# Experts' first layer with one 512-column product for the high and low parts of the tokens

## The chip, the cores and the metric

The kernel runs on one core of one Trainium2 chip. The metric is device time in microseconds (us) for one execution, as the median of several runs.

## What is computed

A recurrence over 768 steps (4 batches, 8 heads of 48) gives 3072 rows of 384 numbers, and a mixture of experts with one expert per token is applied to them:

```python
for t in range(S):
    y[:, :, t] = einsum('bhd,bhde->bhe', r_t, state + (u * k_t) v_t^T)
    state = w_t[..., None] * state + k_t v_t^T
x = y.transpose(0, 2, 1, 3).reshape(3072, 384)
do_compute = x @ w_skip > 0              # the other rows pass through
e_idx = argmax(x @ w_gate)               # 8 experts
h = maximum(x[mask] @ w1[e], 0.0)        # 384 -> 1024
y[mask] = gate_w * (h @ w2[e])           # 1024 -> 384
out[do_compute] = x + y
```

## The kernel before

The first half (to about 132 us) is the recurrence in 24 chunks of 128 steps, with the router beside it. Each chunk's rows are stored to `out`; the router then gives each expert a table of up to 256 rows, in two halves of 128. The second half, `expert(e)` for e = 0 to 7 (L808 to L882), works through the experts one after another. Expert 0's first half of rows is done early, so expert 0 here has only its second half. The order on TensorE, ScalarE, VectorE and GpSimd is the order in which the program issues the work (`manual_schedule`); SP issues its transfers in program order too.

All products of an expert are made in three parts for precision: a number is split into a high part (a rounded copy, type fp32r) and a low part (what is left), and high x high, high x low and low x high are summed in PSUM.

**First layer** (experts 1 to 7, L821 to L851). The 1024 hidden units are done in eight blocks of 128, q = 0 to 7. A block is nine products of 256 columns (the 256 tokens): for each of the three pieces kc of the 384 inputs, w1h with xTh (L837), w1h with xTl (L838), w1l with xTh (L839). They are summed in a PSUM tile psH. The psH tiles go round four banks (tags psA0, psA1, psY, psB), so block q uses the bank of block q-4. Then ScalarE makes the high part of the hidden units, hh (L844, with the relu), and VectorE the low part, hl (L849), which is the last to read the bank.

**Weights of the next expert.** SP loads raw weights in pieces of 512 KB (`load_weights`, L84): three for the first layer into a buffer r0, three for the second into r1. They are cut into twelve slices of 128x512; `split_slice` (L92) makes the high part of one on ScalarE (L89, a cast) and the low part on VectorE (L90). Slices 0 to 5 are the first layer's (slice 2 kc + 0 or 1 holds the lower or upper half of the blocks for piece kc), 6 to 11 the second layer's. `more(k)` does k slices: one after each block, two after each half of the second layer. There is one r0 and one r1, so the load for expert e+2 waits until the slices of expert e+1 have been read out of the buffer.

**Tokens.** `tokens(e+1)` (L764) stands between the layers: six transposes on TensorE (L770) and the split of the next expert's tokens into xTh (ScalarE) and xTl (VectorE).

**Second layer** (L857 to L875). For each half j of the tokens, 24 products of 384 columns (L861 to L863); then VectorE computes fin (L870) from psO, the gate and the gathered rows xg, and GpSimd scatters fin to `out` (L775).

**GpSimd's queue.** Rows xg are gathered by GpSimd (L713), a pair of gathers per expert (`pair`). From expert 3 on a pair is paced: it waits for an hh of expert 0 or 1. The pairs of experts 6 and 7 wait for hh 0 and hh 1 of expert 1. Scatters are held back in `first` until all gathers are issued, and the first one waits until they have landed, since both touch `out`.

Of the kernel before, what the change touches and what calls it, by code (L numbers as in the profile page):

```python
# [8 lines left out]
F32 = mybir.dt.float32  # L9
BF16 = mybir.dt.bfloat16  # L10
F32R = mybir.dt.float32r
# [3 lines left out]
AF = mybir.ActivationFunctionType  # L15
ALU = mybir.AluOpType
# [5 lines left out]
P = 128  # L22
# [6 lines left out]
KC = DM // P  # L29
FC = DF // P  # L30
CAP = 256
# [25 lines left out]
def rwkv_moe_kernel(ctx, tc, wrk, wrk0, vN, uP, wgs, wgp, w12, cst, out):  # L57
    nc = tc.nc
# [13 lines left out]
    def wtile(e, k):  # L72
        nm = f"{WN[k]}{e % 2}"
        pool = wset0 if nm in ("w1h1", "w1l1", "w2h0", "w2l0") else wset1[0]
        t = wsp[e, k] = pool.tile([P, KC * DF], F32R, tag=nm, name=f"{nm}_{e}")
        return t
# [11 lines left out]
    def split(dst_h, dst_l, src, eng=None):  # L88
        nc.scalar.copy(dst_h, src)  # L89
        (eng or nc.vector).tensor_tensor(dst_l, src, dst_h.bitcast(F32), op=ALU.subtract)  # L90

    def split_slice(e, i, eng=None):  # L92
        q, cs = i // 6, slice((i % 6) * 512, (i % 6 + 1) * 512)
        for k in (2 * q, 2 * q + 1):
            if (e, k) not in wsp:
                wtile(e, k)
        split(wsp[e, 2 * q][:, cs], wsp[e, 2 * q + 1][:, cs], raws[e, q][:, cs], eng)
# [13 lines left out]
    def drain(g):  # L111
        for _ in g:
            pass
# [11 lines left out]
    def hidden(ps, xT, fc, kc):  # L125
        o = kc * DF + fc * P
        return nc.tensor.matmul(ps, raws[0, 0][:, o:o + P], xT[:, kc], start=(kc == 0),  # L127
                                stop=(kc == KC - 1))

    banks = ExitStack()  # L130
    ps1 = banks.enter_context(tc.tile_pool(name="ps1", bufs=1, space=PSUM))


    with tc.tile_pool(name="att", bufs=2) as att, \
# [477 lines left out]
        with tc.manual_schedule():  # L612
# [3 lines left out]
            for s in range(-2, n + 1):  # L616
# [73 lines left out]
                k = s + 1 - W_AT  # L690
# [19 lines left out]
        def gather(s, pool):  # L710
            if pool:
                xg[s] = pool.tile([P, DM], F32, tag=f"xg{s}", name=f"xg{s}", bufs=1)
            return nc.gpsimd.indirect_dma_start(  # L713
                out=xg[s], out_offset=None, in_=out,
                in_offset=bass.IndirectOffsetOnAxis(ap=idr[:, s % 2, s // 2:s // 2 + 1], axis=0),
                bounds_check=NT - 1, oob_is_err=False)
# [4 lines left out]
        with tc.manual_schedule(engines={nc.tensor.engine, nc.scalar.engine, nc.vector.engine}):  # L721
            todo, due, done = early_expert(), HEAD * STEP, [0]
# [21 lines left out]
    with tc.tile_pool(name="wset1", bufs=1) as ws1, tc.tile_pool(name="moe", bufs=2) as moe, \  # L744
            tc.tile_pool(name="ps2", bufs=1, space=PSUM) as ps2:
        wset1[0] = ws1
        def pair(e, instr=None):
            for s in (2 * e, 2 * e + 1):
                ga = gather(s, moe)
                if instr is not None:  # L750
                    tc.add_manual_dep(ga.ins, instr.ins.name,
                                      mybir.DependencyInfo(mybir.DependencyClass.Sync,
                                                           mybir.DependencyReason.DATA),
                                      reason="pace")
# [3 lines left out]
        later_pairs = list(range(3, E))  # L758
        verdicts = []
        first = []  # L760

        xTs = {}

        def tokens(e):  # L764
            xTh = moe.tile([P, KC, CAP], F32R, tag="xTh", name=f"xTh{e}")
            xTl = moe.tile([P, KC, CAP], F32R, tag="xTl", name=f"xTl{e}")
            for j in range(2):
                ps = ps1.tile([P, KC, P], F32, tag="psT", name=f"psX2{e}_{j}", bufs=2)
                for kc in range(KC):
                    nc.tensor.transpose(ps[:, kc], xg[2 * e + j][:, kc * P:(kc + 1) * P], ident)  # L770
                split(xTh[:, :, j * P:(j + 1) * P], xTl[:, :, j * P:(j + 1) * P], ps)
            xTs[e] = xTh, xTl

        def scatter(s, o):
            sc = nc.gpsimd.indirect_dma_start(  # L775
                out=out, out_offset=bass.IndirectOffsetOnAxis(ap=ids[:, s % 2, s // 2:s // 2 + 1],
                                                               axis=0),
                in_=o, in_offset=None, bounds_check=NT - 1, oob_is_err=False)
            tc.declare_no_dep(sc.ins, group="rows", reason="tokens are scattered to rows of their own")
            tc.add_to_no_dep_group("rows", sc.ins)  # L780
# [27 lines left out]
        def expert(e):  # L808
            todo = []
            if e + 1 < E:  # L810
                todo = list(range(0 if e > 0 else 6, 12))

            def more(k):
                for _ in range(k):
                    if todo:
                        split_slice(e + 1, todo.pop(0))


            h = {}
            nh = FC if e > 0 else FC // 2  # L820
            for q in range(nh):  # L821
                ps = (ps1 if q % 4 < 2 else ps2).tile(
                    [P, CAP], F32, tag=("psA0", "psA1", "psY", "psB")[q % 4], name=f"psH{e}_{q}")
                hh = moe.tile([P, CAP], F32R, tag="hh", name=f"hh{e}_{q}", bufs=NHB)
                hl = moe.tile([P, CAP], F32R, tag="hl", name=f"hl{e}_{q}", bufs=NHB)
                if e == 0:
                    for i in range(2):
                        ts = slice(i * P, (i + 1) * P)
                        for kc in range(KC):
                            hidden(ps[:, ts], xT0[1], 2 * q + i, kc)  # L830
                        h[1, 2 * q + i] = hh[:, ts], hl[:, ts]
                else:
                    w1h, w1l = wsp[e, 0], wsp[e, 1]
                    xTh, xTl = xTs[e]
                    for kc in range(KC):
                        o = kc * DF + q * P
                        nc.tensor.matmul(ps, w1h[:, o:o + P], xTh[:, kc], start=(kc == 0), stop=False)  # L837
                        nc.tensor.matmul(ps, w1h[:, o:o + P], xTl[:, kc], start=False, stop=False)  # L838
                        nc.tensor.matmul(ps, w1l[:, o:o + P], xTh[:, kc], start=False,  # L839
                                         stop=(kc == KC - 1))  # L840
                    for j in range(2):
                        ts = slice(j * P, (j + 1) * P)
                        h[j, q] = hh[:, ts], hl[:, ts]
                act = nc.scalar.activation(hh, ps, AF.Relu)  # L844
                if later_pairs and (e, q) != (0, 0):
                    pair(later_pairs.pop(0), act)
                    while first and not later_pairs:
                        scatter(*first.pop(0))
                nc.vector.scalar_tensor_tensor(hl, ps, 0.0, hh.bitcast(F32),  # L849
                                               op0=ALU.max, op1=ALU.subtract)  # L850
                more(1)  # L851
            if e + 1 < E:
                tokens(e + 1)
            if e == 0:
                first.append((0, fin0))
            w2h, w2l = wsp[e, 2], wsp[e, 3]
            for j in range(1 if e == 0 else 0, 2):  # L857
                pso = ps1.tile([P, DM], F32, tag=("psu", "pss")[j], name=f"psO{e}_{j}")
                for fc in range(FC):
                    o = slice(fc * DM, (fc + 1) * DM)  # L860
                    nc.tensor.matmul(pso, h[j, fc][0], w2h[:, o], start=(fc == 0), stop=False)  # L861
                    nc.tensor.matmul(pso, h[j, fc][0], w2l[:, o], start=False, stop=False)  # L862
                    nc.tensor.matmul(pso, h[j, fc][1], w2h[:, o], start=False,  # L863
                                     stop=(fc == FC - 1))
                more(2)
                if j == 0 and e in (1, 2):
                    (row_tests, verdict)[e - 1]()
                s = 2 * e + j
                o = moe.tile([P, DM], F32, tag="fin", name=f"fin{e}_{j}", bufs=3)
                nc.vector.scalar_tensor_tensor(o, pso, gates[:, j, e:e + 1], xg[s],  # L870
                                               op0=ALU.mult, op1=ALU.add)
                if later_pairs:
                    first.append((s, o))
                else:
                    scatter(s, o)  # L875
                if s == 2 * E - 3:
                    nc.gpsimd.drain()
                    verdicts.append(nc.values_load(flag_i[0:1, 0:1], min_val=0, max_val=2))
            more(12)
            if e + 2 < E:  # L880
                drain(load_weights(e + 2, 0))
                drain(load_weights(e + 2, 1))  # L882
# [170 lines left out]
```

## Time and profile before

| | |
|---|---|
| median of 3 runs | 289.99 us (289.51 to 290.56) |
| the profiled execution's own time | 289.28 us |
| its span, first to last instruction | 287.5 us |
| mean granted TensorE clock | 0.996 |
| TensorE busy | 269.7 us, 94% of the span |
| VectorE busy | 215.6 us, 75% |
| ScalarE busy | 160.7 us, 56% |
| GpSimd busy | 145.6 us, 51% |

The page calls TensorE's matmuls PE and its weight loads PEld, VectorE DVE, ScalarE ACT, GpSimd POOL and SyncE SP. A matmul's duration in a row is longer than its pitch, since matmuls are pipelined: what one costs in a row of them is the distance from its start to the next one's start. "L837" is line 837 of the kernel before. In a row `psH<-xTh,w1h` the tile before the arrow is written and those behind it are read. An entry in brackets at a row's end is the time that the engine sat idle before it, and what ended it.

### The profile page before, as it was taken

How to read it: one execution, taken by the hardware profiler on the slowest of the kernel's cores; microseconds unless marked ns; L12 is line 12 of the kernel's file. 1: busy time of each engine (PE TensorE's matmuls, PEld its weight loads, DVE VectorE, ACT ScalarE, POOL GpSimd, SP SyncE). 2: the span in 40 equal slices, each digit the busy share in tenths (PEclk: the TensorE clock that was granted, in tenths of full speed). 3: DMA queues.
4: the chain of work that ended last, by engine and by line, in shares of the span. 5: the costliest groups of instructions: out<-in, count | busy, mean ns of one | idle time of the engine just before them, and what ended most of it. 6: DMA issues, size and time to landing. Idle time of an engine off the chain costs nothing.

```text
span 287.5 us, 8933 instructions
## 1 busy us (share of the span) xinstructions
PE 269.7 (94%) x3587; PEld 247.9 (86%) x3588; DVE 215.6 (75%) x412; ACT 160.7 (56%) x466; POOL 145.6 (51%) x140
## 2 busy tenths in 40 slices
PE   6899999999999998989889999999999999999993
PEld 2688888878887887877889999999999999999992
DVE  7998899999999999852638596966859578595420
ACT  5266656786767855967327481835728367282310
POOL 4987775699979996983566635011020110301111
PEclk9999999999999999999999999999999999999998
DMA  7999999987998779962365997566562656600001
GB/s 221 225 319 354 332 324 378 357 255 245 280 330 263 240 239 377 275 219 84 126 214 167 359 342 240 199 227 235 198 231 78 235 225 217 247 25 27 8 3 43
DMA packets 26131, 64.41 MB, mean 224 GB/s; under 512 B 4342, under 2 KB 15386, under 8 KB 26080
## 3 DMA queue, kind: packets, MB, share of 16 engines
q1 hardware_dynamic: 23712, 58.14, 60.9%
q0 software_dynamic: 2048, 5.48, 5.8%
q8 instruction: 30, 0.49, 0.7%
q10 hardware_dynamic: 320, 0.13, 0.2%
q14 instruction: 21, 0.17, 0.2%
HBM read 56.69 MB, written 7.86 MB: 225 GB/s over the span
## 4 chain that ended last, share of the span: by engine, by line
issue 33%; PE 11%; POOL 6%; DVE 4%; ACT 2%; DMA 1%; POOLq 1%; DVEq 0%
POOL out L775 5%; PE psH L127 2%; DMA xg<-out,idr 1%; PE psH L839 1%; PE psH L838 1%; PE psH L837 1%; DVE w2l L90 1%; PE psY L395 1%; PE psA L344 1%; PE psY L363 1%; ACT w1h L107 1%; PE psO L862 0%; PE psO L861 0%; PE psO L863 0%; DVE hot L488 0%
## 5 line engine op out<-in xcount | busy, mean ns | idle before, releaser
L775 POOL DMA_INDIRECT out<-fin,ids x16 | 16.8, 1048 | 99.8 <-DVE fin L870 94.0
L844 ACT ACTIVATE hh<-psH 128x256 fp32r<-128x256 f32 x60 | 23.0, 384 | 57.6 <-PE psH L839 54.3
L839 PE MATMUL psH<-xTh,w1l 128*128 128x256 f32 x168 | 47.5, 283 | 0.0
L838 PE MATMUL psH<-xTl,w1h 128*128 128x256 f32 x168 | 47.5, 283 | 0.0
L837 PE MATMUL psH<-xTh,w1h 128*128 128x256 f32 x168 | 47.5, 283 | 0.0
L861 PE MATMUL psO<-w2h,hh 128*128 128x384 f32 x120 | 40.9, 341 | 0.0
L863 PE MATMUL psO<-w2h,hl 128*128 128x384 f32 x120 | 40.2, 335 | 0.0
L862 PE MATMUL psO<-w2l,hh 128*128 128x384 f32 x120 | 40.1, 334 | 0.0
L312 POOL TENSOR_TENSOR kq<-wrk,q 128x512 f32<-128x512 f32 x24 | 28.4, 1184 | 13.9 <-DVE q L295 5.2
L350 DVE TENSOR_TENSOR asb<-psA,c_sb 128x512 f32<-128x512 f32 x48 | 30.5, 677 | 4.7 <-PE psA L344 4.6
L849 DVE SCALAR_TENSOR_TENSOR hl<-psH,hh 128x256 fp32r<-128x256 f32 x60 | 25.2, 420 | 11.5 <-ACT hh L844 10.0
L317 DVE TENSOR_TENSOR_SCAN rh<-wrk,rowsk,pss 128x520 f32<-128x520 f32 x24 | 31.1, 1296 | 3.2 <-PE pss L537 1.0
L295 DVE TENSOR_TENSOR_SCAN q<-wrk,pss 128x520 f32<-128x520 f32 x24 | 29.6, 1232 | 3.6 <-DMA wrk<-wrk 1.1
L839 PEld LDWEIGHTS psH<-xTh,w1l 128*128 128x128 f32 x168 | 32.2, 192 | 0.0
L838 PEld LDWEIGHTS psH<-xTl,w1h 128*128 128x128 f32 x168 | 32.2, 192 | 0.0
L837 PEld LDWEIGHTS psH<-xTh,w1h 128*128 128x128 f32 x168 | 32.2, 191 | 0.0
L304 POOL TENSOR_TENSOR rk<-wrk 128x512 f32<-128x512 f32 x24 | 31.2, 1298 | 0.8 <-DMA wrk<-wrk 0.8
L322 POOL TENSOR_TENSOR rp<-wrk,rh 128x512 f32<-128x512 f32 x23 | 27.3, 1187 | 6.0 <-DVE rh L317 5.5
L395 PE MATMUL psY<-asb,v 128*48 128x128 f32 x384 | 26.5, 276 | 3.8 <-DVE psY L367 3.8
L870 DVE SCALAR_TENSOR_TENSOR fin<-psO,gates,xg 128x384 f32<-128x384 f32 x15 | 9.3, 618 | 27.4 <-PE psO L863 23.1
L90 DVE TENSOR_TENSOR w2l<-r,w2h 128x512 fp32r<-128x512 f32 x42 | 27.8, 687 | 0.9
L344 PE MATMUL psA<-rp,kq 64*64 64x64 f32 (+1 forms) x768 | 25.8, 251 | 2.2 <-DVE rp L322 1.4
(151 smaller groups left out, 603.7 us busy)
## 6 DMA issues: line engine op xcount, KB each, us to landing
r<-w SPq DMA_DIRECT2D x48, 512.0 KB
wrk<-wrk SPq DMA_DIRECT2D x21, 772.5 KB
v<-vN SPq DMA_DIRECT2D x24, 192.0 KB
vt<-wrk SPq DMA_DIRECT2D x48, 96.0 KB
out<-x SPq DMA_DIRECT2D x24, 192.0 KB
wrk<-wrk SPq DMA_DIRECT2D x1, 579.4 KB
wrk<-wrk SPq DMA_DIRECT2D x1, 512.0 KB
wrk<-wrk SPq DMA_DIRECT2D x1, 384.0 KB
```

The costliest lines, as they stand in the source:

```text
L90: (eng or nc.vector).tensor_tensor(dst_l, src, dst_h.bitcast(F32), op=ALU.subtract)
L295: nc.vector.tensor_tensor_scan(q.rearrange("p a j -> p (a j)")[:, ::-1], t[:, 1:1 + n_][:, ::-1], ones_at[:, 1:1 + n_][:, ::-1], 0.0, op0= ...
L304: nc.gpsimd.tensor_tensor(work[i]["rk"].rearrange("p a j -> p (a j)"), t[:, R_OFF:K_OFF], t[:, K_OFF:V_OFF], op=ALU.mult)
L317: nc.vector.tensor_tensor_scan(rh.rearrange("p a j -> p (a j)"), wk["w"][:, 0:NP * CW], reads_at[:, :NP * CW], rowsk, op0=ALU.mult, op1=AL ...
L350: nc.vector.tensor_tensor(s, psa[g], tri.rearrange("p (o j) -> p o j", o=1).to_broadcast([P, NP, P]), op=ALU.mult)
L775: sc = nc.gpsimd.indirect_dma_start(out=out, out_offset=bass.IndirectOffsetOnAxis(ap=ids[:, s % 2, s // 2:s // 2 + 1], axis=0), in_=o, in_ ...
L837: nc.tensor.matmul(ps, w1h[:, o:o + P], xTh[:, kc], start=(kc == 0), stop=False)
L838: nc.tensor.matmul(ps, w1h[:, o:o + P], xTl[:, kc], start=False, stop=False)
L839: nc.tensor.matmul(ps, w1l[:, o:o + P], xTh[:, kc], start=False, stop=(kc == KC - 1))
L861: nc.tensor.matmul(pso, h[j, fc][0], w2h[:, o], start=(fc == 0), stop=False)
L862: nc.tensor.matmul(pso, h[j, fc][0], w2l[:, o], start=False, stop=False)
L863: nc.tensor.matmul(pso, h[j, fc][1], w2h[:, o], start=False, stop=(fc == FC - 1))
```

## The change

In the first layer the tokens' high and low parts lie side by side in one tile xT. One product of w1h with both, 512 columns wide, takes the place of L837 and L838 and fills a whole bank: its left half collects high x high, its right half high x low. The product of w1l with the high part is added into the left half. ScalarE copies the right half to SBUF (`side`), and VectorE adds it to the left half in PSUM; then hh and hl follow as before, out of a function `finish`, which is called one block later. The splitting of the next expert's weights moves: in the first layer of experts 1 to 6 one slice after every second block (0, 2, 4, 6), the first of them on VectorE and the low parts of the other three on GpSimd, and four instead of two after each half of the second layer.

```diff
         def tokens(e):
-            xTh = moe.tile([P, KC, CAP], F32R, tag="xTh", name=f"xTh{e}")
-            xTl = moe.tile([P, KC, CAP], F32R, tag="xTl", name=f"xTl{e}")
+            xT = moe.tile([P, KC, 2, CAP], F32R, tag="xT", name=f"xT{e}")
+            xTh, xTl = xT[:, :, 0], xT[:, :, 1]
...
-            def more(k):
+            def more(k, eng=None):
                 for _ in range(k):
                     if todo:
-                        split_slice(e + 1, todo.pop(0))
+                        split_slice(e + 1, todo.pop(0), eng)
+
+            def finish(q, ps, hh, hl):
+                act = nc.scalar.activation(hh, ps, AF.Relu)
+                if later_pairs and (e, q) != (0, 0):
+                    pair(later_pairs.pop(0), act)
+                    while first and not later_pairs:
+                        scatter(*first.pop(0))
+                nc.vector.scalar_tensor_tensor(hl, ps, 0.0, hh.bitcast(F32),
+                                               op0=ALU.max, op1=ALU.subtract)
+                if e == 0 or q % 2 == 0:
+                    more(1, nc.gpsimd if e > 0 and q > 0 else None)
 
-            h = {}
+            h, due = {}, []
             nh = FC if e > 0 else FC // 2
             for q in range(nh):
-                ps = (ps1 if q % 4 < 2 else ps2).tile(
-                    [P, CAP], F32, tag=("psA0", "psA1", "psY", "psB")[q % 4], name=f"psH{e}_{q}")
+                both = (ps1 if q % 4 < 2 else ps2).tile(
+                    [P, 2, CAP], F32, tag=("psA0", "psA1", "psY", "psB")[q % 4], name=f"psH{e}_{q}")
+                ps = both[:, 0]
...
                     for kc in range(KC):
                         o = kc * DF + q * P
-                        nc.tensor.matmul(ps, w1h[:, o:o + P], xTh[:, kc], start=(kc == 0), stop=False)
-                        nc.tensor.matmul(ps, w1h[:, o:o + P], xTl[:, kc], start=False, stop=False)
-                        nc.tensor.matmul(ps, w1l[:, o:o + P], xTh[:, kc], start=False,
-                                         stop=(kc == KC - 1))
+                        nc.tensor.matmul(both, w1h[:, o:o + P], xT[:, kc], start=(kc == 0),
+                                         stop=(kc == KC - 1), skip_group_check=True)
+                        nc.tensor.matmul(ps, w1l[:, o:o + P], xT[:, kc, 0], start=False,
+                                         stop=(kc == KC - 1), skip_group_check=True)
+                    side = moe.tile([P, CAP], F32, tag="side", name=f"side{e}_{q}")
+                    nc.scalar.copy(side, both[:, 1])
+                    nc.vector.tensor_tensor(ps, ps, side, op=ALU.add)
...
-                act = nc.scalar.activation(hh, ps, AF.Relu)
-                if later_pairs and (e, q) != (0, 0):
-                    pair(later_pairs.pop(0), act)
-                    while first and not later_pairs:
-                        scatter(*first.pop(0))
-                nc.vector.scalar_tensor_tensor(hl, ps, 0.0, hh.bitcast(F32),
-                                               op0=ALU.max, op1=ALU.subtract)
-                more(1)
+                due.append((q, ps, hh, hl))
+                if e == 0 or q > 0:
+                    finish(*due.pop(0))
+            while due:
+                finish(*due.pop(0))
...
-                more(2)
+                more(4)
```

On ScalarE, at the beginning of expert 2's first layer, the order before was (hh is the high part of the hidden units, w1h_3 the high part of expert 3's first-layer weights, r_30 the raw ones):

```order
L844 ACTIVATE hh_0_3163<-psH_0_3162 128x256
L89 CAST w1h_3_3176<-r_30_3154 128x512
L844 ACTIVATE hh_1_3181<-psH_1_3180 128x256
L89 CAST w1h_3_3176<-r_30_3154 128x512
L844 ACTIVATE hh_2_3197<-psH_2_3196 128x256
```

and now it is:

```order
L854 COPY side_0_3169<-psH_0_3160 128x256
L854 COPY side_1_3181<-psH_1_3172 128x256
L820 ACTIVATE hh_0_3161<-psH_0_3160 128x256
L89 CAST w1h_3_3186<-r_30_3152 128x512
L854 COPY side_2_3199<-psH_2_3190 128x256
L820 ACTIVATE hh_1_3173<-psH_1_3172 128x256
```

The cast of slice 0 now stands ahead of the copy of block 2 and of hh 1.

On GpSimd, from expert 1 on, the order before was scatters alone (fin_73 and fin_1_2898 are expert 0's two halves):

```order
L775 DMA out<-fin_73,ids 3072x384
L775 DMA out<-fin_1_2898,ids 3072x384
L775 DMA out<-fin_0_3115,ids 3072x384
L775 DMA out<-fin_1_3149,ids 3072x384
L775 DMA out<-fin_0_3341,ids 3072x384
```

and now it is (w1l_2 is the low part of expert 2's first-layer weights, r_20 the raw ones):

```order
L775 DMA out<-fin_73,ids 3072x384
L775 DMA out<-fin_1_2897,ids 3072x384
L90 TENSOR_TENSOR w1l_2_2942<-r_20_2899,w1h_2_2941 128x512 x3
L775 DMA out<-fin_0_3109,ids 3072x384
L775 DMA out<-fin_1_3147,ids 3072x384
L90 TENSOR_TENSOR w1l_3_3187<-r_30_3152,w1h_3_3186 128x512 x3
```

Three low parts per expert stand between the scatters of the expert before and its own. On SP, the load of expert 3's raw first-layer weights had these waits before:

```order
L84 DMA r_30_3154<-w 128x1024 [waits DMAHW1_49,DMAHW2_49,DMAHW0_49,DVE_49]
L84 DMA r_30_3154<-w 128x1024 x2
```

and has these now:

```order
L84 DMA r_30_3152<-w 128x1024 [waits DMAHW1_49,DMAHW0_49,DMAHW2_49,DVE_49,Pool_49]
L84 DMA r_30_3152<-w 128x1024 x2
```

GpSimd (Pool) has come in beside VectorE among those that the load waits for.

## Rows read from the trace of the kernel before

**Rows 1.** Busy time by stretch, PE to POOL; then granted clock, DMA share, GB/s

```profile
149.00:282.30 133.30, 133.30 (x959) 132.95 (x958) 90.28 (x178) 67.96 (x152) 28.72 (x27) 1.00 0.51 180
212.60:221.20 8.60, 8.60 (x73) 8.60 (x73) 7.17 (x14) 6.30 (x14) 0.98 (x1) 1.00 0.48 181
```

**Rows 2.** Timeline of PE: expert 0's second layer, experts 1 and 4 (start, us, engine, line)

```profile
155.33 0.34 PE L862 MATMUL psO<-w2l,hh 128*128 128x384 f32 x1
...
159.15 0.33 PE L863 MATMUL psO<-w2h,hl 128*128 128x384 f32 x1
159.32 0.28 PE L837 MATMUL psH<-xTh,w1h 128*128 128x256 f32 x1
...
212.59 0.28 PE L837 MATMUL psH<-xTh,w1h 128*128 128x256 f32 x1
...
221.21 0.82 PE L770 MATMUL psX<-c_sb,xg 128*128 128x128 f32 x6
...
230.21 0.28 PE L837 MATMUL psH<-xTh,w1h 128*128 128x256 f32 x1
```

**Rows 3.** Timeline of PE, warm-up products (the second is the third after the first)

```profile
5.28 0.59 PE L610 MATMUL psw<-warm 128*128 128x512 bf16 x2
...
5.92 0.59 PE L610 MATMUL psw<-warm 128*128 128x512 bf16 x2
```

**Rows 4.** Timeline of ACT, first activation of expert 4

```profile
213.85 0.38 ACT L844 ACTIVATE hh<-psH 128x256 fp32r<-128x256 f32 x1 [6.34 <-PE psH L839]
```

**Rows 5.** Groups by line: VectorE's product in PSUM, of the recurrence

```profile
L367 DVE TENSOR_TENSOR psY<-psY,vt 128x512 f32<-128x512 f32 x24 | 16.6, 690 | 0.0
```

**Rows 6.** Timeline of ACT, then of DVE, expert 1

```profile
161.70 0.39 ACT L844 ACTIVATE hh<-psH 128x256 fp32r<-128x256 f32 x1 [4.31 <-PE psH L839]
161.98 0.61 ACT L89 CAST w1h<-r 128x512 fp32r<-128x512 f32 x1
162.49 0.39 ACT L844 ACTIVATE hh<-psH 128x256 fp32r<-128x256 f32 x1
...
161.57 0.62 DVE L870 SCALAR_TENSOR_TENSOR fin<-psO,gates,xg 128x384 f32<-128x384 f32 x1 [3.13 <-PE psH L839]
162.12 0.43 DVE L849 SCALAR_TENSOR_TENSOR hl<-psH,hh 128x256 fp32r<-128x256 f32 x1
162.62 0.69 DVE L90 TENSOR_TENSOR w1l<-r,w1h 128x512 fp32r<-128x512 f32 x1
163.23 0.42 DVE L849 SCALAR_TENSOR_TENSOR hl<-psH,hh 128x256 fp32r<-128x256 f32 x1
163.57 0.68 DVE L90 TENSOR_TENSOR w1l<-r,w1h 128x512 fp32r<-128x512 f32 x1
```

**Rows 7.** Timeline of POOL (low parts, gathers, scatters) and the PE row that waited

```profile
136.51 3.71 POOL L108 TENSOR_TENSOR w1l<-r,w1h 128x512 fp32r<-128x512 f32 x3 [0.97 <-ACT w1h L107]
143.80 1.21 POOL L713 DMA_INDIRECT xg<-out,idr  x1 [3.58 <-DMA r<-w]
...
147.95 0.52 PE L572 MATMUL psX<-c_sb,xg 128*128 128x128 f32 x3 [0.86 <-DMA xg<-out,idr]
...
166.73 1.23 POOL L713 DMA_INDIRECT xg<-out,idr  x1 [0.30 <-issue]
173.15 1.02 POOL L775 DMA_INDIRECT out<-fin,ids  x1 [5.19 <-DVE good L790]
174.47 1.00 POOL L775 DMA_INDIRECT out<-fin,ids  x1 [0.30 <-DVE vt L799]
```

**Rows 8.** Timeline of SP: issues of raw weights

```profile
140.25 0.34 SPq L84 DMA_DIRECT2D r<-w  x1
...
168.05 1.46 SPq L84 DMA_DIRECT2D r<-w  x2
...
220.90 0.33 SPq L84 DMA_DIRECT2D r<-w  x1
```

**Rows 9.** DMA queues from 168 to 172 us: packets, MB, share of 16 engines

```profile
q1 hardware_dynamic: 194, 0.71, 49.7%
q0 software_dynamic: 176, 0.51, 40.6%
```

More of the change, by code (lines that the diff above doesn't have):

```diff
@@ L771, in tokens @@
                 split(xTh[:, :, j * P:(j + 1) * P], xTl[:, :, j * P:(j + 1) * P], ps)
-            xTs[e] = xTh, xTl
+            xTs[e] = xT
         def scatter(s, o):
@@ L833, in expert @@
                     w1h, w1l = wsp[e, 0], wsp[e, 1]
-                    xTh, xTl = xTs[e]
+                    xT = xTs[e]
                     for kc in range(KC):
                         o = kc * DF + q * P
-                        nc.tensor.matmul(ps, w1h[:, o:o + P], xTh[:, kc], start=(kc == 0), stop=False)
-                        nc.tensor.matmul(ps, w1h[:, o:o + P], xTl[:, kc], start=False, stop=False)
-                        nc.tensor.matmul(ps, w1l[:, o:o + P], xTh[:, kc], start=False,
-                                         stop=(kc == KC - 1))
+                        nc.tensor.matmul(both, w1h[:, o:o + P], xT[:, kc], start=(kc == 0),
[5 more added lines that the diff above has]
+                    nc.vector.tensor_tensor(ps, ps, side, op=ALU.add)
                     for j in range(2):
```

## The prediction

> **What bounds the kernel now.** I read the busy times by stretch first. From 149.0 to 282.3 us TensorE is busy all the time, at a granted clock of 1.00 (the full 2.4 GHz), while VectorE is busy 68% and ScalarE 51% of it [rows 1]; in an expert's first layer VectorE has 7.17 of 8.60 us. Next the timeline of TensorE. Expert 4 begins at 212.59, ends its first layer at 221.21 and hands over to expert 5 at 230.21 [rows 2]: 8.62 us for 72 products of 256 columns, one per 119.7 ns, with no gap. So here the end of the kernel is a sum of product pitches, and whatever shortens a pitch shortens the kernel, as long as nobody makes TensorE wait. The start and the recurrent part are the same in both orders and drop out.
>
> **The products.** What has to be known is the pitch of a 512-column product of this type; the trace has none. It has 256 columns at 119.7 ns and 384 columns at (159.15 - 155.33)/22 = 173.6 ns [rows 2], so 128 columns more cost 53.9 ns, and 512 columns come to 173.6 + 53.9 = 227.5 ns. Two bounds: twice the short one, 239.4 ns (nothing saved), and the bf16 512-column warm-up products, (5.92 - 5.28)/3 = 213 ns [rows 3]. I take 227.5, because the 384-column row is of the same type with a weight load each and is the nearest. One merge saves 239.4 - 227.5 = 11.9 ns; 24 per expert and seven experts make 168: **-2.0 us** (0 to -4.4 by the bounds). The 168 weight loads that go are overlapped by products and gain nothing of their own.
>
> What does a fixed cost per product look like elsewhere? The Trainium skill ("TensorE: Matmul & The Clock Gate", section "Back-to-back issue gap") gives a gap of N / 2.4 + 2.5 ns; 256 columns would take 109.2 ns, against 119.7 in the trace. By that page a merge would save 2.5 ns and all of them an estimated 0.42 us. The sum here does not use it.
>
> **The added work and the ring of four banks.** Per block of 128 hidden units there is one more copy on ScalarE (the side, PSUM to SBUF, 128x256: like the 0.38 us activation of that size [rows 4]) and one more add on VectorE in PSUM. A 128x512 VectorE product in PSUM takes 690 ns [rows 5]; at half the columns I take 0.43, close to the 0.42 of the hl row [rows 6], with 0.38 and 0.69 as ends. Three of the four low parts that the first layer still splits go to GpSimd at 1.26 us each. By load this fits: on one engine the next instruction starts 0.28 us after an activation and 0.51 after a cast, 0.34 after hl and 0.61 after a low part [rows 6]; ScalarE has 16 x 0.28 + 4 x 0.51 = 6.5 us and VectorE 16 x 0.35 + 0.61 = 6.2 us in a layer of 8 x 1.04 = 8.34 us.
>
> The latency is tighter. A bank is written by TensorE, read by side, rewritten by the add, read by hh and hl, and TensorE wants it back four blocks later. Before, hh starts 1.26 us after the layer's start [rows 4], 0.18 after the next block begins; a hop from ScalarE to VectorE costs 0.03 [rows 6]. In the new order, from the layer's start: side 1 at 2 x 1.04 + 0.18 = 2.26, hh 0 at 2.54, the cast of slice 0 at 2.82, its low part on VectorE 3.48; side 2 at 3.34; add 2 behind the low part at 4.09; hl 1 at 4.44, over at 4.86. TensorE asks for bank 1 at 5.21: a margin of 0.3 us. The later blocks come out at 0.6. No wait in an ordinary expert.
>
> Expert 1 is not ordinary. Its first activation starts at 161.70 and fin at 161.57, 1.1 us later than 159.32 + 1.26 [rows 2, 6]; the old order, with one step fewer in the ring, absorbed it. In the new one: side 0 at 2.38, add 0 2.80, hh 0 3.27, cast 3.55, low part 4.21, add 2 4.82, hl 1 from 5.17 to 5.59, bank back at 5.64 against 5.21: **+0.4 us** (0 if the late start does not recur).
>
> **What is moved past a queue.** This is the step I weigh most. In expert 1 GpSimd's queue holds four gathers, which wait for hh 0 and hh 1, then two scatters, which wait until the gathers have landed. The three low parts of expert 2 now stand behind those scatters; they were on VectorE. Before, the last gather was started at 166.73 and took 1.23 us, and the first scatter started at 173.15 [rows 7]. Two things hang on the three low parts. TensorE needs slice 2 at the second low product of expert 2. And SP's load of expert 3's raw first-layer weights goes into the buffer they read, so it waits for the third; before, it was issued at 168.05 [rows 8], right behind the sixth low part on VectorE.
>
> In the new order hh 0 of expert 1 ends at 159.32 + 3.65 = 162.97; the gathers follow at 1.3 us and the last is over at 168.1 to 168.8. When does it land? The fastest seen is 2.9 us (end of the 143.80 gather to the product that waited for it at 147.95), the slowest the 5.2 to the scatter at 173.15 [rows 7]. So the first scatter starts between 171.3 and 174.0. I take 172.0, nearer the early end: from 168 to 172 the weight load took 49.7% of the DMA engines beside the gathers' 40.6% [rows 9], and in the new order that load is not there yet. Two scatters at 1.3 and three low parts, the row of three taking 3.71 us [rows 7], end at 172.0 + 2.6 + 3.7 = 178.3 (177.6 to 180.3). A raw piece is ready 3.2 us after its issue (issue at 140.25 [rows 8]; the gather at 143.80 that waited for it, less 0.3): 181.5.
>
> Expert 2 starts at 159.32 + 17.62 - 0.29 + 0.43 = 177.1 and wants to cast slice 0 at 177.1 + 2.82 = 179.9. ScalarE takes its work in order, so side 2 stands behind that cast, add 2 and hl 1 behind side 2; bank 1 is free 2.1 us after the piece: 183.6, and TensorE wants it at 177.1 + 5.21 = 182.3: **+1.3 us** (0.6 to 3.3). Slice 2's low part, at 177.1, is in time for 177.7, barely.
>
> From expert 2 on the scatters come later than the low parts, so GpSimd is free. The raw load of an expert's successor is issued when slices 4 and 5 are split, behind the tokens, some 12.6 us into the expert (before: 8.3, at 220.90 [rows 8]), and is wanted 20.2 us in: with 3.2 us to land that costs nothing; without those 4 us of cover each expert would stall as expert 2 does. The second raw half is issued behind fin as before and wanted 3 us later than before: nothing.
>
> **Sum.** -2.0 + 0.4 + 1.3 = -0.3 us, on the profiled execution's 289.28 us 289.0; the median of the runs is 289.99, 0.7 above it, so I predict 289.7 us. **No change that can be measured**: 0.3% of the time, 0.87 us, is what a measurement here can tell from none.
>
> **Rivals.**
> - **The late load does not show (faster).** If gathers land fast, or GpSimd's third low part is over by 177.0, only expert 1's wait is left: -1.6 us, 288.4; without that wait too, 288.0. For it: the DMA engines are emptier then. Against it: even 2.9 us of landing leaves 0.6 us of wait. Chance 0.32, with the partial forms of it that still gain over 0.87.
> - **The late load shows fully (slower).** Gathers land as late as before: low parts over at 180.3, expert 2 waits 3.3 us, sum +1.7, 291.7. It decides from 179.5 on for the third low part. For it: the gathers start 0.9 us later than before and their own backlog is the same. Chance 0.18.
> - **The pitch goes by columns, nothing is fixed (slower).** 512 columns take 239 ns; then only the waits are left: +1.7, 291.7. The 384-column row speaks against it (it would be 179.6, and is 173.6). A page's 2.5 ns, above, would make 291.3 of it. Chance 0.08.
> - The forecast, within 0.87 us of before: 0.42.
>
> A fourth, inside the slower ones: the in-place add costs its 512-wide 0.69 us. Then the 0.3 us margin of every expert goes too.
>
> **Numbers.** Faster 0.32, same 0.42, slower 0.18 + 0.08 = 0.26. The range runs from the two clean forms (288.0) to just under the two slow ones (291.6), with the tails of each, at most 0.2, left outside.
>
> **What would show it.** The 512-column product starts 227 ns before its follower; the first layers of experts 3 to 7 take 8.34 us without a gap. TensorE has one gap of some 0.4 us at block 5 of expert 1 and one of 1.3 us at block 5 of expert 2. GpSimd's three low parts of expert 2 start behind two scatters at about 174.6, and SP issues the following raw load at 178.3. Wrong I would be if that load is issued before 177 or its cast does not hold ScalarE, if the gaps recur in each expert, or if the 512-column pitch is 213 or 239.

## The result and the profile after

The changed kernel takes **292.81 us** (median of 6 runs, 292.42 to 293.32) against 290.27 for the kernel before (6 runs): a ratio of 1.0088, 95% interval 1.0067 to 1.0109. It is slower by 2.5 us, above the forecast of 289.7 and outside the range of 288.0 to 291.6. The profiled execution took 292.42 us with a span of 290.6 and a mean granted clock of 0.989 (before: 289.28, 287.5, 0.996).

First the groups by line of the changed kernel (line, engine, operation, count | busy us, mean ns of one | idle time ahead and its releaser). They answer to [rows 4, 5]:

```profile
L849 PE MATMUL psH<-xT,w1h 128*128 128x512 f32 x168 | 60.7, 402 | 3.0 <-DVE hl L825 2.7
L855 DVE TENSOR_TENSOR psH<-psH,side 128x256 f32<-128x256 f32 x56 | 23.9, 431 | 17.3 <-ACT side L854 16.6 <-issue 0.5 <-ACT w1h L89 0.2
L854 ACT COPY side<-psH 128x256 f32<-128x256 f32 x56 | 21.0, 376 | 40.5 <-PE psH L851 37.1 <-ACT side L854 2.7 <-issue 0.4
L795 DVE TENSOR_SCALAR good<-gall 128x24 f32<-128x24 f32 x1 | 4.1, 4149 | 0.0
```

All 168 merged products are there, and the added copy (376 ns) and add (431 ns) cost what was put in the sum. The odd row is the last: a VectorE instruction on 128x24 numbers that took 4149 ns.

The timeline of PE, which answers to [rows 2] (start, us, engine, line; idle time and releaser in brackets), in experts 2 and 3:

```profile
176.56 0.39 PE L849 MATMUL psH<-xT,w1h 128*128 128x512 f32 x1
176.79 0.28 PE L851 MATMUL psH<-xT,w1l 128*128 128x256 f32 x1
176.91 0.39 PE L849 MATMUL psH<-xT,w1h 128*128 128x512 f32 x1
177.38 0.39 PE L851 MATMUL psH<-xT,w1l 128*128 128x256 f32 x1
...
181.02 0.28 PE L851 MATMUL psH<-xT,w1l 128*128 128x256 f32 x1
184.04 0.50 PE L849 MATMUL psH<-xT,w1h 128*128 128x512 f32 x1 [2.74 <-DVE hl L825]
...
185.08 0.28 PE L851 MATMUL psH<-xT,w1l 128*128 128x256 f32 x1
185.48 0.80 PE L849 MATMUL psH<-xT,w1h 128*128 128x512 f32 x1
...
186.28 0.63 PE L849 MATMUL psH<-xT,w1h 128*128 128x512 f32 x1
186.71 0.41 PE L851 MATMUL psH<-xT,w1l 128*128 128x256 f32 x1
...
188.84 0.39 PE L849 MATMUL psH<-xT,w1h 128*128 128x512 f32 x1
...
190.25 0.49 PE L770 MATMUL psX<-c_sb,xg 128*128 128x128 f32 x3
...
199.65 0.39 PE L849 MATMUL psH<-xT,w1h 128*128 128x512 f32 x1
...
207.97 0.82 PE L770 MATMUL psX<-c_sb,xg 128*128 128x128 f32 x6
```

Expert 3's first layer takes 207.97 - 199.65 = 8.32 us, as do those of experts 4 to 7. Expert 2's takes 190.25 - 176.56 = 13.69. Of the excess of 5.37, 0.24 lie where the second low product came 0.47 instead of 0.23 us behind its neighbour, **2.90** at the gap ahead of block 4 (181.02 to 184.04, less a pitch of 0.12) and 2.05 behind that gap (184.04 to 190.25 is 6.21 for half a layer, 4.16 elsewhere); 0.18 are small pieces. Of the 2.05, 0.28 are a second, short wait, at block 5 (185.08 to 185.48, less the pitch). The five pairs of products behind it, 185.48 to 188.84, took 3.36 us in place of 5 x 0.347 = 1.73: **1.63**, the largest part. What that is shows in the windows (us; busy time and count of PE, PEld, DVE, ACT, POOL; granted clock, DMA share, GB/s):

```profile
184.00:186.00 2.00, 1.85 (x7) 1.42 (x8) 1.94 (x5) 1.72 (x7) 0.04 (x1) 0.85 0.96 332
186.00:188.00 2.00, 2.00 (x8) 1.64 (x7) 0.84 (x3) 0.72 (x4) 1.28 (x1) 0.50 0.99 389
```

Behind the gap the granted clock fell to 0.50, the lower of its two levels, and a 512-column product took 0.43 us from its start to the next instead of 0.23.

Who made TensorE wait? The timelines of POOL, SP, DVE and ACT, which answer to [rows 6 to 8]:

```profile
172.43 1.02 POOL L775 DMA_INDIRECT out<-fin,ids  x1 [4.93 <-DVE w1l L90]
173.76 1.00 POOL L775 DMA_INDIRECT out<-fin,ids  x1 [0.30 <-DVE good__2774 L788]
174.78 3.78 POOL L90 TENSOR_TENSOR w1l<-r,w1h 128x512 fp32r<-128x512 f32 x3
...
178.59 21.50 SPq L84 DMA_DIRECT2D r<-w  x12
...
174.46 4.15 DVE L795 TENSOR_SCALAR good<-gall 128x24 f32<-128x24 f32 x1
...
179.22 0.62 DVE L882 SCALAR_TENSOR_TENSOR fin<-psO,gates,xg 128x384 f32<-128x384 f32 x1
179.75 2.49 DVE L90 TENSOR_TENSOR w2l<-r,w2h 128x512 fp32r<-128x512 f32 x4
182.16 0.61 DVE L882 SCALAR_TENSOR_TENSOR fin<-psO,gates,xg 128x384 f32<-128x384 f32 x1
182.69 0.75 DVE L855 TENSOR_TENSOR psH<-psH,side 128x256 f32<-128x256 f32 x2
183.56 0.42 DVE L825 SCALAR_TENSOR_TENSOR hl<-psH,hh 128x256 fp32r<-128x256 f32 x1
...
185.01 0.41 DVE L825 SCALAR_TENSOR_TENSOR hl<-psH,hh 128x256 fp32r<-128x256 f32 x1
...
183.14 0.38 ACT L820 ACTIVATE hh<-psH 128x256 fp32r<-128x256 f32 x1 [3.50 <-DVE psH L855]
183.42 0.61 ACT L89 CAST w1h<-r 128x512 fp32r<-128x512 f32 x1
```

The three low parts ran where the prediction had put them, behind two scatters (174.78, forecast 174.6), and the load behind them was issued at 178.59 (forecast 178.3). But ScalarE's cast at 183.42 follows hh without a wait for DMA: the load was not the last to come. VectorE was. Its small instruction of L795, one of the tests that the program makes on its tables between the halves of expert 1's second layer, stood from 174.46 to 178.61, until GpSimd's low parts were over. Behind it fin, four low parts, the second fin, the adds and hl 0 came late, and TensorE's first bank with them. The short wait at block 5 is for the second bank: hl 1, behind hh 0, the cast and side 2, ended at 185.42.

### The profile page after: what moved, and what is told of

Same layout as the page of the kernel before. It is cut to its first block, busy times and chain, and to the rows that moved or that the text cites. A ratio compares the mean times of both kernels' runs of the same rounds, so it can differ in the third digit from the quotient of the medians.

```text
span 290.6 us, 8759 instructions
## 1 busy us (share of the span) xinstructions
PE 271.5 (93%) x3419; PEld 240.3 (83%) x3420; DVE 227.4 (78%) x450; ACT 174.9 (60%) x522; POOL 171.9 (59%) x158
## 4 chain that ended last, share of the span: by engine, by line
PE 34%; issue 9%; DVE 6%; POOL 5%; ACT 4%; DMA 1%; POOLq 1%; DVEq 0%; ACTq 0%
PE psH L849 9%; PE psH L851 5%; PE psO L873 4%; PE psO L875 4%; PE psO L874 4%; PE psH L127 2%; POOL out L775 2%; DMA xg<-out,idr 1%; POOL w1l L90 1%; DVE w2l L90 1%; PE psX L770 1%; ACT w1h L89 1%; ACT hh L820 1%; PE psY L395 1%; PE psA L344 1%
## 5 line engine op out<-in xcount | busy, mean ns | idle before, releaser
L849 PE MATMUL psH<-xT,w1h 128*128 128x512 f32 x168 | 60.7, 402 | 3.0 <-DVE hl L825 2.7
L775 POOL DMA_INDIRECT out<-fin,ids x16 | 20.6, 1290 | 50.6 <-DVE fin L882 36.5
L851 PE MATMUL psH<-xT,w1l 128*128 128x256 f32 x168 | 47.8, 284 | 0.1
L854 ACT COPY side<-psH 128x256 f32<-128x256 f32 x56 | 21.0, 376 | 40.5 <-PE psH L851 37.1
L849 PEld LDWEIGHTS psH<-xT,w1h 128*128 128x128 f32 x168 | 32.2, 192 | 10.8 <-DVE hl L825 3.5
L90 POOL TENSOR_TENSOR w1l<-r,w1h 128x512 fp32r<-128x512 f32 x18 | 23.1, 1291 | 25.8 <-issue 16.7
L855 DVE TENSOR_TENSOR psH<-psH,side 128x256 f32<-128x256 f32 x56 | 23.9, 431 | 17.3 <-ACT side L854 16.6
L851 PEld LDWEIGHTS psH<-xT,w1l 128*128 128x128 f32 x168 | 32.4, 193 | 0.4 <-POOL w1l L90 0.4
L404 ACT COPY xT<-psY 128x512 f32<-128x512 f32 x24 | 14.0, 583 | 23.3 <-PE psY L399 18.9
L90 DVE TENSOR_TENSOR w2l<-r,w2h 128x512 fp32r<-128x512 f32 x42 | 26.7, 685 | 0.3
```

Source lines behind the costliest of these rows:

```text
L849: nc.tensor.matmul(both, w1h[:, o:o + P], xT[:, kc], start=(kc == 0), stop=(kc == KC - 1), skip_group_check=True)
L851: nc.tensor.matmul(ps, w1l[:, o:o + P], xT[:, kc, 0], start=False, stop=(kc == KC - 1), skip_group_check=True)
```

## The experiments

Two theories. **A**: VectorE is held while GpSimd works, and its backlog holds the bank. **B**: the late load holds ScalarE's cast, as predicted. Both start from the same place, the three low parts behind the scatters in expert 1. All ratios are against the kernel before, run on the same chip.

**1. Take the cause away: expert 1's low parts on VectorE.**

```diff
-                    more(1, nc.gpsimd if e > 0 and q > 0 else None)
+                    more(1, nc.gpsimd if e > 1 and q > 0 else None)
```

> Expert 1's three low parts go back from GpSimd to VectorE, experts 2 to 6 keep theirs on GpSimd. Both theories: no gap in expert 2, since neither VectorE is held nor the load late; the load is issued before 175. VectorE has 1.8 us more to do in expert 1's first layer, so the wait there may grow from 0.5 to about 1 us. 288.0 to 289.0 us. If the gap in expert 2 stays, both theories fall.

Measured: 289.83 us (10 runs), ratio 0.9973 [0.9939, 1.0007], above the forecast of 288.0 to 289.0. All seven first layers take 8.32 or 8.33 us and no gap is left; the load is issued at 173.51. So the loss in expert 2 hangs on these three instructions. From expert 1's start to the last product the second half is 2.1 us shorter than before; the profiled execution reached expert 1 at 160.56 (before 159.32), and the ratio alone doesn't tell a gain.

**2. Theory A alone: three other GpSimd products in the low parts' place, that read nothing the load waits for.**

```diff
-                    more(1, nc.gpsimd if e > 0 and q > 0 else None)
+                    more(1, nc.gpsimd if e > 1 and q > 0 else None)
+                    if e == 1 and q > 0:
+                        nc.gpsimd.tensor_tensor(h0h[:, 4:], h0l[:, :4].bitcast(F32),
+                                                h0h[:, :4].bitcast(F32), op=ALU.subtract)
```

> As e2, and in the place of the three low parts GpSimd does three products of the same size on tiles that nobody else uses any more, so nothing waits for them. Theory A: VectorE's row tests are held again for up to 4 us though no load is late; TensorE has a gap of 2 to 3.5 us in expert 2 and the half clock behind it, 291 to 293 us. Theory B: as e2, within 0.3 us of it.

Measured: 293.41 us (10 runs), ratio 1.0096 [1.0060, 1.0131]. Timelines of DVE, POOL and PE:

```profile
175.16 1.76 DVE L799 SCALAR_TENSOR_TENSOR vt<-vt 128x1 f32<-128x1 f32 x1
...
177.38 4.35 DVE L90 TENSOR_TENSOR w2l<-r,w2h 128x512 fp32r<-128x512 f32 x4
...
175.60 4.38 POOL L830 TENSOR_TENSOR h0h<-h0l,h0h 128x512 fp32r<-128x512 f32 x3
...
183.53 0.80 PE L852 MATMUL psH<-xT,w1h 128*128 128x512 f32 x1 [2.65 <-DVE hl L825]
```

The load was issued at 172.20, early, and expert 2's first layer still took 12.61 us: 2.82 of wait and 1.47 at half clock. The hold fell on other instructions than in the changed kernel (L799, and four low parts at 4.35 us in place of 2.49), with the same end. A is enough, and the time came out just above its forecast of 291 to 293.

**3. Theory B alone: low parts on VectorE as in 1, the load of expert 3 held back by a tiny product that reads the raw buffer.**

```diff
...
+                    if (e, q) == (2, 1):
+                        late = ps1.tile([P, 512], F32, tag="psT", name="pslate", bufs=2)
+                        nc.tensor.matmul(late[:, :4], identb, raws[2, 0][:, :4].bitcast(BF16)[:, 1::2],
+                                         start=True, stop=True)
+                        drain(load_weights(3, 0))
+                        drain(load_weights(3, 1))
...
-            if e + 2 < E:
+            if e + 2 < E and e != 1:
```

> Edit: the kernel with expert 1's low parts on VectorE (289.83 us, expert 2's first layer 8.32), but expert 3's raw loads are held back until TensorE has done two blocks of expert 2: a product of 4 columns there reads the raw buffer, so the load is issued about 2.1 us after expert 2's start, as in the changed kernel (178.59 - 176.56 = 2.0). Slices, VectorE and GpSimd are on time, so the late load stands alone. Theory (the prediction's chain, cast of slice 0 late, side 2, add 2 and hl 1 behind it): with the 3.2 us to a ready piece that I had used, the piece is ready 5.3 us after the expert's start, the bank 2.1 us later at 7.4 against 5.2, a wait of 2.2 us at block 5; with the 4.4 us seen where VectorE was free and the load late (issued 181.41, cast at 185.85), a wait of 3.4 us. First layer 10.5 to 11.8 us, perhaps half clock behind it; time 291.8 to 294. Rival (a late load is absorbed, and the changed kernel lost its time to VectorE's hold alone): first layer 8.3 to 8.7 us, time 289.5 to 290.3.

Measured: 293.49 us (10 runs), ratio 1.0105 [1.0074, 1.0135]. Timelines of SP, ACT and PE:

```profile
179.24 20.92 SPq L84 DMA_DIRECT2D r<-w  x12
...
183.45 0.62 ACT L89 CAST w1h<-r 128x512 fp32r<-128x512 f32 x1 [3.50 <-DMA r<-w]
...
182.20 0.28 PE L851 MATMUL psH<-xT,w1l 128*128 128x256 f32 x1
185.52 0.50 PE L849 MATMUL psH<-xT,w1h 128*128 128x512 f32 x1 [3.04 <-DVE hl L825]
```

The chain of the prediction is there as written: the wait is at block 5, and the bank came back 185.52 - 183.45 = 2.07 us after the cast began (forecast 2.1). But the piece took 183.45 - 179.24 = 4.2 us, not 3.2. So B alone makes TensorE wait 3.2 us (182.20 to 185.52, less the pitch), and half clock follows here too: the layer took 13.38 us, where 10.5 to 11.8 had been expected. The load was issued 2.3 us into expert 2, against 2.0 in the changed kernel. B is enough as well. In the changed kernel the two lay over each other, and A ended a little later: with the 4.2 us seen here the piece was ready at an estimated 182.8, and ScalarE reached the cast at 183.42.

**4. The tests moved one expert on, so that VectorE is free.**

```diff
-                if j == 0 and e in (1, 2):
-                    (row_tests, verdict)[e - 1]()
+                if j == 0 and e in (2, 3):
+                    (row_tests, verdict)[e - 2]()
```

> The row tests (VectorE, ten small instructions) move from expert 1 to expert 2 and the verdict from 2 to 3; nothing else changes. Theory A (VectorE was held: in the changed kernel one 128x24 TENSOR_SCALAR of the row tests lasted 4.15 us, until GpSimd's three low parts were over, and everything behind it on VectorE came late): VectorE begins expert 2 on time, no gap above 0.5 us at block 5, about 288.0 to 288.6 us. Theory B (the raw load of expert 3, issued behind GpSimd's third low part, is late): the load is still issued at about 178.5, its first piece is ready 3.2 us later, ScalarE's cast waits for it and TensorE has a gap of about 2 us at block 5 of expert 2, with some loss of clock behind it: 290.5 to 292.

Measured: 294.25 us (4 runs), ratio 1.0139 [1.0068, 1.0210]; expert 2's first layer 13.87 us; both forecasts (288.0 to 288.6 and 290.5 to 292) were missed. VectorE was not held, and still nothing was gained:

```profile
175.11 2.52 POOL L775 DMA_INDIRECT out<-fin,ids  x1 [0.30 <-DVE w2l L90]
177.65 3.74 POOL L90 TENSOR_TENSOR w1l<-r,w1h 128x512 fp32r<-128x512 f32 x3
...
180.20 0.39 PE L851 MATMUL psH<-xT,w1l 128*128 128x256 f32 x1 [2.18 <-POOL w1l L90]
...
185.85 0.62 ACT L89 CAST w1h<-r 128x512 fp32r<-128x512 f32 x1 [2.76 <-DMA r<-w]
...
187.92 0.50 PE L849 MATMUL psH<-xT,w1h 128*128 128x512 f32 x1 [1.23 <-DVE hl L825]
```

VectorE's four low parts now ran beside the second scatter, which took 2.52 us instead of the 1.00 of the changed kernel, so the low parts started at 177.65. Slice 2 was late for the second low product, and the load (issued 181.41) for the cast. Moving the victim away leaves the cause.

**5. The moves alone, without the merged product, the copy and the add.** The edit is the kernel before with the new `more` and `split_slice` places and engines only:

```diff
...
-                more(1)
+                if e == 0 or q % 2 == 0:
+                    more(1, nc.gpsimd if e > 0 and q > 0 else None)
...
-                more(2)
+                more(4)
```

> Edit: the kernel before, three products of 256 columns and no add, with only the new places and engines of the splitting (one slice after blocks 0, 2, 4, 6, low parts of three of them on GpSimd in experts 1 to 6, four after each half of the second layer). Tells whether the moves cost by themselves. Theory (the hold of VectorE is enough without the new step in the ring of banks): low parts behind the scatters from about 175 to 179, VectorE's row tests held for some 4 us, hl of block 0 of expert 2 over at about 183, TensorE without a bank for 1 to 2 us at block 4, perhaps half clock behind it: 291.5 to 293.5. Rival (the new side copy and add, and finish one block later, made the ring too short; the old ring has some 2 us of slack): no gap over 0.3 us in expert 2, time 290.0 to 290.7.

Measured: 292.62 us (6 runs), ratio 1.0081 [1.0053, 1.0109]. Experts 1 and 3 to 7 take 8.62 or 8.63 us, expert 2 takes 12.10, in the profiled execution (294.81 us, the longest of the six) by a late slice 2 and a late bank. Timelines of PE and DVE:

```profile
180.86 0.39 PE L839 MATMUL psH<-xTh,w1l 128*128 128x256 f32 x1 [1.07 <-POOL w1l L90]
...
187.80 0.38 PE L837 MATMUL psH<-xTh,w1h 128*128 128x256 f32 x1 [1.74 <-DVE hl L849]
...
177.42 6.39 DVE L90 TENSOR_TENSOR w2l<-r,w2h 128x512 fp32r<-128x512 f32 x4
```

Here L795 was not held (0.17 us), but the four low parts were: 6.39 us, against 2.49. So the moves lose 3.5 us in expert 2 without the merge and its longer ring. The changed kernel lost 5.37; whether the ring has a share in the difference is not shown.

**6. Keep TensorE busy in the wait.** 26 products of 256 bf16 columns that nobody reads, first ahead of block 5, then ahead of block 4, of expert 2:

```diff
+                    if (e, q) == (2, 4):
+                        psw = ps1.tile([P, 512], F32, tag="psT", name="pskeep", bufs=2)
+                        for _ in range(26):
+                            nc.tensor.matmul(psw[:, :2 * P], identb, iota, start=True, stop=True)
```

> The changed kernel, with 26 products of 256 columns (bf16, 107 ns each, 2.8 us) on TensorE ahead of block 5 of expert 2, in the place of the idle time. Theory: the wait for VectorE is the same, but the granted clock stays at 1.00 and the products behind it go at 227 and 120 ns instead of 430 and 210; expert 2's first layer falls from 13.7 to 11.3 us and the kernel to 290.4 us. Rival (the slow pitch behind the gap is not the clock but late weights or transfers): the pitch stays at 430, 292.8 us.

> Edit: the changed kernel with 26 filler products of 256 bf16 columns (some 2.8 us) on TensorE ahead of block 4 of expert 2, where the changed kernel waits 2.9 us for the first bank; their result is read by nobody. Theory (of the 5.4 us that expert 2 loses, 2.0 come from the granted clock at half behind that wait, not from a wait): the filler lies in the wait, the products behind it start every 0.227 and 0.120 us, granted clock 1.00 from 184 to 191, expert 2's first layer about 11.6 us instead of 13.7, time 290.6 to 291.2. Rival (the slow pitches are of other origin, such as late operands): pitches of 0.43 and 0.21 stay, time 292.8 or above.

Measured: 295.46 us (4 runs), ratio 1.0169 [1.0095, 1.0244], and 292.96 us (4 runs), ratio 1.0104 [1.0065, 1.0144]. Both times missed the forecast (290.4, and 290.6 to 291.2); the second lies where its rival put it (292.8 or above), but without the slow pitches that the rival asked for. In the first the waits came earlier, at slice 2 (0.87 us idle) and block 4 (2.03), so the filler was plain extra work. In the second it lay in the wait, and the windows answer to those of the changed kernel:

```profile
184.00:186.00 2.00, 2.00 (x18) 1.62 (x16) 1.80 (x5) 1.21 (x4) 0.99 (x1) 1.00 0.98 320
186.00:188.00 2.00, 1.88 (x11) 1.40 (x10) 1.75 (x6) 1.72 (x6) 0.19 (x1) 1.00 0.95 350
```

The last four blocks took 4.66 us, against 6.21 in the changed kernel, at a granted clock of 1.00. That the half clock costs some 1.6 us behind such a wait is borne out; that a filler pays is not: in that execution the low parts began 1.15 us ahead of expert 2 instead of 1.78, slice 2 cost 0.9 us instead of 0.24, and the median did not fall. From expert 1's start to the last product the execution was 1.3 us shorter than that of the changed kernel, but it reached expert 1 that much later (160.09 against 158.74).

**7. Why the moves came with the merge: the merge with the old splitting.** One slice after each block on VectorE, two after each half of the second layer:

```diff
-                if e == 0 or q % 2 == 0:
-                    more(1, nc.gpsimd if e > 0 and q > 0 else None)
+                more(1)
...
-                more(4)
+                more(2)
```

> Edit: the changed kernel with the splitting where it was before: one slice after each block on VectorE, two after each half of the second layer. Tells why the moves came with the merge. Theory (VectorE would then be the limit of the first layer): per block an add 0.35, a low half 0.34 and a low part 0.61 us give 1.30 us against TensorE's 1.04; the first layers of experts 1 to 6 take 9.5 to 10.4 us with gaps that end on VectorE, expert 7's 8.3; time 296 to 301. Rival (VectorE has room for all of it): first layers of 8.3 us everywhere, time 288.2 to 289.5.

Measured: 290.27 us (10 runs), ratio 1.0001 [0.9973, 1.0028]. The forecast of 296 to 301 was far off, and the rival's 288.2 to 289.5 was missed as well. One block of VectorE in expert 3:

```profile
201.22 0.41 DVE L825 SCALAR_TENSOR_TENSOR hl<-psH,hh 128x256 fp32r<-128x256 f32 x1
...
202.48 0.41 DVE L825 SCALAR_TENSOR_TENSOR hl<-psH,hh 128x256 fp32r<-128x256 f32 x1
```

VectorE does need 202.48 - 201.22 = 1.26 us per block against TensorE's 1.04, as I had reckoned. But the excess of 0.22 a block adds up to 1.8 us over a layer, and the ring of four banks takes most of it: the layers of experts 2 to 6 took 8.63 or 8.64 us (expert 1's 9.00), only 0.3 over 8.32, and the second layer pays the backlog off. These 0.3 are what the merge saves: with the old splitting the layers take as long as before the change, so without moving the splitting the merge gains nothing. I had priced the layer by the rate of its slowest engine, which holds for a long loop and not for eight blocks.

**8. The low parts ahead of the scatters.** The scatters are released in expert 1's second layer, no longer with the last pair of gathers:

```diff
                     pair(later_pairs.pop(0), act)
-                    while first and not later_pairs:
-                        scatter(*first.pop(0))
...
                 else:
+                    while first:
+                        scatter(*first.pop(0))
                     scatter(s, o)
```

> Edit: the changed kernel, but expert 0's two scatters are no longer released with the last pair of gathers; they are issued after expert 1's first half of the second layer, so GpSimd's three low parts of expert 2 stand ahead of them and do not wait for the gathers to land. Nothing else moves. Theory (both losses follow from the low parts' place behind the scatters): the low parts are over at about 171.5 us, the raw load of expert 3 is issued near 172.5, VectorE's row tests at 174.5 find no GpSimd product beside them (the long one of the changed kernel took 4.15 us, here under 0.5), expert 2's first layer takes 8.3 us without a gap, no stretch at half clock; second half as short as with the low parts on VectorE, 2.1 us under before; time 288.2 to 289.8 depending on the first half. Rival (work of GpSimd beside VectorE costs wherever it lies): expert 1's first layer grows by 1 us or more, as VectorE's adds and low halves lie beside the low parts, time near 291.

Measured: **288.29 us** (12 runs, 286.89 to 289.82), ratio 0.9938 [0.9914, 0.9962]: below both kernels, and inside the forecast of 288.2 to 289.8. Timelines of POOL, SP and DVE:

```profile
166.94 1.00 POOL L713 DMA_INDIRECT xg<-out,idr  x1 [0.30 <-issue]
167.96 3.80 POOL L90 TENSOR_TENSOR w1l<-r,w1h 128x512 fp32r<-128x512 f32 x3
173.75 1.28 POOL L775 DMA_INDIRECT out<-fin,ids  x1 [1.99 <-DVE w1l L90]
...
172.99 22.41 SPq L84 DMA_DIRECT2D r<-w  x12
...
175.22 0.17 DVE L795 TENSOR_SCALAR good<-gall 128x24 f32<-128x24 f32 x1
```

The low parts use the time in which GpSimd waited for the gathers anyway; the test of L795 takes 0.17 us, and expert 2's first layer 8.55. The three instructions are the same as in the changed kernel, on the same engine; only their place in the queue differs.

## Why the prediction was wrong

- **The products** (-2.0 us): right. 8.32 us over 24 pairs is 346.7 ns a pair, less 119.7 for the low product 227.0 ns, forecast 227.5. Seven experts gain 0.30 each, 2.1 us. At 256, 384 and 512 columns the pitches are 119.7, 173.6 and 227.0 ns, each 13 to 14 ns above its columns at 2.4 GHz; the 2.5 ns of the formula that the prediction quotes and leaves out of its sum is not borne out here.
- **The added work and the ring**: right. The add took 0.43 us, and experts 3 to 7 have no gap.
- **Expert 1** (+0.4): right in the changed kernel, whose first side started at 161.05 and whose layer took 8.82, 0.50 over the others. It does not come each time: 8.31 to 8.33 us in five of the other runs with the merge, 8.50 to 9.00 in three. What delays the handover was not followed up.
- **What is moved past a queue** (+1.3, 0.6 to 3.3): **this step failed**, by its size and by what ended the wait. The place and times of the low parts and of the load's issue held to 0.3 us. But the term priced one chain, the late load; expert 2 lost 5.37 us, and the cast did not hold ScalarE, which the prediction itself names as a sign of being wrong. (1) Its landing was taken from one row, 3.2 us; here it was 4.2 (experiment 3) and 4.4 (experiment 4), and the load alone makes 3.2 us of wait. Why it is longer is not shown; SP issued three pieces in a row in the one case and six in the others. (2) I asked what is queued behind the moved instructions and who reads the buffer, and not what runs beside them on VectorE: experiment 2 shows that this alone makes 2.8. In the changed kernel it ended last. (3) Half clock behind the wait, 1.6 us, stood in no term. (4) Slice 2 was "in time, barely"; it was late by 0.24.
- **The range** ended at 291.6, just under the rival in which the late load shows fully (3.3 us, 291.7). With 2.9 us of wait that rival was the nearest in size, but by luck: its condition, low parts over at 180.3, did not come (178.56), and it, too, ended at the wait and had no slow clock behind it.
- **The raw loads from expert 3 on** (nothing): right, no gap.

The sum as measured: -2.1 + 0.5 + 5.37 = +3.8 us; expert 1 began 0.58 earlier than in the profile of before (158.74 against 159.32), which leaves 3.2, and the profiled executions differ by 292.42 - 289.28 = 3.14.

On (2), the Trainium skill ("SBUF — State Buffer", section "Who interferes with whom") says that VectorE and GpSimd share one pair of SBUF ports under an exclusive lock, which a `tensor_scalar` in a two-port mode, or a VectorE instruction with two SBUF inputs beside a GpSimd one that reads SBUF, needs too; whoever comes second waits for the whole instruction. The runs agree that both kinds are held (L795 at 4.15 us against 0.17, four low parts at 4.35 against 2.49); whether L795 ran in a two-port mode no view shows. The runs differ from it in two things. L795 stood through three GpSimd products, not one; and by the rows it began 0.32 us ahead of the first of them, while the second scatter still stood on GpSimd. That a port is what they wait for is the Trainium skill's account; the runs show that the hold comes with GpSimd's products and goes with them.

## What to carry to other kernels

When work moves to another engine's queue, price three things: what it now waits behind, who waits for it, and what the engines beside it do while it runs. A term for a wait of TensorE should ask what the granted clock does behind it (here 1.5 to 1.6 us more behind waits of 2.2 to 3.0 us), and a landing time should be taken from more than one row. Here the cure was not to take the move back but to give the moved work an earlier place in the same queue.

## What the runs showed of the hardware

- GpSimd's products hold VectorE. Beside three of them a 128x24 `tensor_scalar` took 4.15 us (alone 0.17) and four VectorE low parts took 4.35 us in experiment 2 and 6.39 in experiment 5 (alone 2.49). Which instruction is caught differs between executions.
- VectorE's low parts hold a scatter only at times. Begun some 0.36 us into four low parts, it took 1.18 us in most rows and 2.99 in others, both in the changed kernel (at 231.64 and 266.30). The held ones, and the 2.52 us of experiment 4, ended 0.86 to 0.88 us behind the last low part. What decides between the two is not shown.
- Behind waits of 2.74, 2.65, 2.18 and 3.04 us (the changed kernel, experiments 2, 4 and 3) the granted clock fell to 0.50, and its slow pitches cost 1.5 to 1.6 us more; behind waits of 2.03 us (the first filler run) and 1.74 us (experiment 5) it stayed at 1.00.
- A raw piece of 512 KB was ready 4.2 and 4.4 us after its issue in experiments 3 and 4, against 3.2 us worked out from the profile of before.
